# VectorE's part of a first-layer step emitted behind the next step's evacuations

## The chip, the cores and the metric

One Trainium2 chip, one of its cores. The metric is the device time of one execution in microseconds (us), taken without the profiler unless said; the profile's span is some 2 us shorter than that time (243.4 beside 245.14 in the profiled execution of the kernel before). A program on one core has no die to compare with, so executions are told apart by their span and by the mean clock granted to TensorE, which the records give for every execution.

## The reference

Chunked attention (4 batches, 8 heads, 768 rows of 64; chunks of 32 queries see 16 rows to the left, 8 to the right and 8 memory rows), then a two-layer MLP on the 3072 x 512 result:

```python
x = attention(q, k, v, mem_k, mem_v)       # (3072, 512)
h = x @ w_in                               # 512 -> 2048
s = np.sin(alpha * h)
g = h + s * s / (alpha + 1e-09)
out = g @ w_out                            # 2048 -> 512
```

## The kernel before

Matmul and transpose results land in PSUM, the memory that TensorE writes; a buffer there is free again once an engine has copied or used up what it holds (its evacuation). The kernel works through four blocks, one per batch. For each there is an attention burst that fills xT, then the first layer in 16 steps (ft), each of which makes 128 rows of g; the second layer of the block is a stream of matmuls handed out in small portions between other work. In the first layer of blocks 1 and 2 the q and k of the *next* block are transposed as well, one piece every other step. The PSUM buffers in use are three two-bank ones ("big") and two one-bank ones ("sm"). hT is a step's first-layer result, tt_a a transpose, kTi and qT the copies made of it, o and o_sb a second-layer output and its copy; hT 14 or sin 9 below is that of ft 14 or 9.

```python
big = ctx.enter_context(tc.tile_pool(name="big", bufs=3, space=bass.MemoryType.PSUM))
smp = ctx.enter_context(tc.tile_pool(name="smp", bufs=2, space=bass.MemoryType.PSUM))
# ...
def t_k(kb, hp):                            # piece for k; t_q is the same with a copy on ScalarE
    t = t_tile()                            # in blocks 1 and 2: tt_a, from the two "sm" buffers
    # ... six transposes on TensorE into t ...
    nc.vector.tensor_copy(kTi[...], t[...])             # large
    # ... and two small tensor_copy, all three on VectorE
# ...
def l1(i, ft, xT, gT, sq, split=False):     # the case without split
    hT = big.tile([P, 2, 512], F32, name="hT", tag="big")
    # ... 8 matmuls into hT ...
    nc.scalar.activation(u[:], hT[:, :, 0:HALF], ACTF.Sin, scale=alpha_sb[:, ft:ft + 1])
    if sq == "A":
        nc.scalar.activation(s2[:], u[:], ACTF.Square)
    else:
        (nc.vector if sq == "D" else nc.gpsimd).tensor_tensor(
            out=s2[:], in0=u[:], in1=u[:], op=ALU.mult)
    nc.vector.scalar_tensor_tensor(         # gT = s2 / alpha + hT, releases hT
        out=gv, in0=s2[:], scalar=inv_alpha[:, ft:ft + 1],
        in1=hT[:, :, 0:HALF], op0=ALU.mult, op1=ALU.add)
# ...
def l2(i, gT, last=False):
    for s in range(NSUB):
        o = smp.tile([P, d_model], F32, name="o", tag="sm")
        # ... 16 matmuls into o, handed out one by one ...
        if s % 2 == 0:
            nc.vector.tensor_copy(o_sb[:], o[:])        # releases o
        else:
            nc.scalar.copy(o_sb[:], o[:])
# ...
for ft in range(FT):
    sq = ("ADADADAAADADADAA" if i == 0 else "ADAAPDADADAPADAD")[ft]
    if 1 <= ft:
        stream.take(3 if last else 2)       # second-layer matmuls, and o_sb when one is full
    if 0 < i < B - 1 and ft in at_ft:       # ft even
        piece(at_ft[ft])                    # k at ft = 0, 4, 8, 12; q between
    # ...
    l1(i, ft, xT, gT, sq, i == 0 and ft in (3, 7, 11))
```

The order in which instructions are written is the order in which each engine gets them.

The softmax here doesn't subtract the row's maximum and nothing guards it: scores larger than these inputs give would overflow.

Of the kernel before, what the change touches and what calls it, by code (L numbers as in the profile page):

```python
# [9 lines left out]
P = 128  # L10
# [6 lines left out]
ALU = mybir.AluOpType  # L17
# [28 lines left out]
def kernel(  # L46
# [12 lines left out]
    nc = tc.nc  # L59
    B, H, S, D = q.shape  # L60
# [8 lines left out]
    HALF = S // 2  # L69
# [28 lines left out]
    inv_alpha = consts.tile([P, FT], F32, name="inv_alpha")  # L98
# [13 lines left out]
    def load_qk(b):  # L112
        kb, qb = alloc_qk()
        for src, dst in ((k, kb), (q, qb)):
            nc.gpsimd.dma_start(
                dst[:].rearrange("p h r d -> p h (r d)"),
                src[b].rearrange("h (p r) d -> p h (r d)", p=P),
            )
        return kb, qb
# [32 lines left out]
    def put_memv(b):  # L152
        nc.vector.tensor_copy(
            vws[b % 2][64:72, :, :, 0:D],
            memv_st[64:72, b].unsqueeze(2).to_broadcast([NM, H, NJ, D]),
        )

    def put_memk(b):
        nc.vector.tensor_copy(
            kTi[:, :, 24:KW].rearrange("p g (j c) -> p g j c", c=104)[:, :, :, 40:40 + NM],  # L160
            memkT[:, :, NM * b:NM * b + NM].unsqueeze(2).to_broadcast([P, HP, NJ, NM]),
        )
# [28 lines left out]
    for c0, c1, thr, val in (  # L191
# [4 lines left out]
            out=biasm[:, c0:c1], in_=biasm[:, c0:c1],  # L196
# [27 lines left out]
    def pair_up(src, hp, eng=None):  # L224
        pr = blk.tile([P, 6, 2, D], BF, name="pr")
        (eng or nc.gpsimd.tensor_copy)(  # L226
            pr[:].rearrange("p r e d -> p e r d"), src[:, 2 * hp:2 * hp + 2]
        )
        return pr
# [81 lines left out]
    def burst(b, stream, shares, lag):  # L311

        xT = xp.tile([P, KT, S], BF, name="xT")
        ptl, xbl = {}, {}
        for s in range(NJ + lag + 1):
            n = shares[s] if s < len(shares) else 0
            if s < NJ:
                ptl[s] = qk_exp(s)
            if b == 0:
                spin(1)  # L320
            stream.take(n // 3, True)
            if 0 <= s - lag < NJ:
                xbl[s - lag] = pv(b, s - lag, ptl.pop(s - lag))
                if b == 0:
                    xbl[s - lag] = (xbl[s - lag][0], None)
            stream.take((n + 1) // 3, True)
            if 0 <= s - lag - 1 < NJ:
                xt(xT, s - lag - 1, *xbl.pop(s - lag - 1))
            stream.take((n + 2) // 3, True)
        return xT  # L330


    def l1(i, ft, xT, gT, sq, split=False):
        if split:
            hts = [smp.tile([P, 512], F32, name="hs", tag="sm") for _ in range(2)]
        else:
            hT = big.tile([P, 2, 512], F32, name="hT", tag="big")
            hts = [hT[:, 0], hT[:, 1]]
        for kt in range(KT):
            for hf in range(2):  # L340
                nc.tensor.matmul(  # L341
                    hts[hf][:, 0:HALF],
                    w_in_sb[:, kt, P * ft:P * ft + P],
                    xT[:, kt, HALF * hf:HALF * hf + HALF],
                    start=(kt == 0), stop=(kt == KT - 1),
                )
        u = mlp.tile([P, 2, HALF], F32, name="u")
        if split:
            for hf in range(2):
                nc.scalar.activation(  # L350
                    u[:, hf], hts[hf][:, 0:HALF], ACTF.Sin, scale=alpha_sb[:, ft:ft + 1])
        else:
            nc.scalar.activation(u[:], hT[:, :, 0:HALF], ACTF.Sin, scale=alpha_sb[:, ft:ft + 1])  # L353
        s2 = mlp.tile([P, 2, HALF], F32, name="s2")
        if sq == "A":
            nc.scalar.activation(s2[:], u[:], ACTF.Square)  # L356
        else:
            (nc.vector if sq == "D" else nc.gpsimd).tensor_tensor(  # L358
                out=s2[:], in0=u[:], in1=u[:], op=ALU.mult)
        gv = gT[:, ft, :].rearrange("p (e c) -> p e c", e=2)  # L360
        for hf in range(2):
            if split:
                nc.vector.scalar_tensor_tensor(
                    out=gv[:, hf], in0=s2[:, hf], scalar=inv_alpha[:, ft:ft + 1],
                    in1=hts[hf][:, 0:HALF], op0=ALU.mult, op1=ALU.add)
            elif hf == 0:
                nc.vector.scalar_tensor_tensor(  # L367
                    out=gv, in0=s2[:], scalar=inv_alpha[:, ft:ft + 1],
                    in1=hT[:, :, 0:HALF], op0=ALU.mult, op1=ALU.add)

    def l2(i, gT, last=False):
        for s in range(NSUB):
            o = smp.tile([P, d_model], F32, name="o", tag="sm")
            end = last and s == NSUB - 1
            o_sb = mlp.tile([P, d_model], F32, name="o_sb")
            row = S * i + P * s
            if end:
                oh = [o, smp.tile([P, d_model], F32, name="o", tag="sm")]
                for c in range(2):
                    cs = slice(256 * c, 256 * c + 256)  # L380
                    for ft in range(FT):
                        nc.tensor.matmul(  # L382
                            oh[c][:, 0:256], gT[:, ft, P * s:P * s + P], w_out_sb[:, ft, cs],
                            start=(ft == 0), stop=(ft == FT - 1),
                        )
                    if c == 0:
                        nc.scalar.copy(o_sb[:, cs], oh[c][:, 0:256])
                    else:
                        nc.vector.tensor_copy(o_sb[:, cs], oh[c][:, 0:256])
                    nc.sync.dma_start(out[row:row + P, cs], o_sb[:, cs])  # L390
            else:
                for ft in range(FT):
                    nc.tensor.matmul(  # L393
                        o[:], gT[:, ft, P * s:P * s + P], w_out_sb[:, ft, :],
                        start=(ft == 0), stop=(ft == FT - 1),
                    )
                    if ft < FT - 1:
                        yield False
                if s % 2 == 0:
                    nc.vector.tensor_copy(o_sb[:], o[:])  # L400
                else:
                    nc.scalar.copy(o_sb[:], o[:])  # L402
                nc.sync.dma_start(out[row:row + P, :], o_sb[:])
            yield True
# [31 lines left out]
    xT = burst(0, stream, (), 2)  # L436
# [3 lines left out]
    for i in range(B):  # L440
        gT = gp.tile([P, FT, S], BF, name="gT")
        last = i == B - 1
        at_ft = {2 * n: n for n in range(8)}
        pieces = []
        if not last:
            srcs = [(kq_next[n % 2], n // 2) for n in range(2 * HP)]
        state["pools"] = 1

        def pair_to(n):
            while len(pieces) < min(n, 2 * HP):  # L450
                pieces.append(pair_up(*srcs[len(pieces)], nc.vector.tensor_copy if i == 0 and len(pieces) % 2 == 0 else None))

        def piece(n):
            pair_to(n + 3)
            (t_k if n % 2 == 0 else t_q)(pieces[n], n // 2)

        if 0 < i < B - 1:
            pair_to(2)
        for ft in range(FT):
            sq = ("ADADADAAADADADAA" if i == 0 else "ADAAPDADADAPADAD")[ft]  # L460
            if 1 <= ft:
                stream.take(3 if last else 2)
            if 0 < i < B - 1 and ft in at_ft:
                piece(at_ft[ft])
            if i == 0 and ft == 14:
                pair_to(3)
            l1(i, ft, xT, gT, sq, i == 0 and ft in (3, 7, 11))
        stream.add(l2(i, gT, last))
        if not last:
            if i == 0:  # L470
                state["pools"], state["t"] = 3, 0
                stream.take(4)
                for n in range(2 * HP):
                    piece(n)
                    stream.take(3, True)
            if i + 2 < B:
                kq_next = load_qk(i + 2)
            if i == 0:
                xT = burst(i + 1, stream, (3, 3, 3, 4, 4, 4, 4, 4, 4, 4, 5, 5), 3)
            else:  # L480
                xT = burst(i + 1, stream, (16, 8, 6, 6, 6, 5, 5, 5, 5, 5), 1)
            if i + 2 < B:
                put_memk(i + 2)
            stream.take(3)
            if i + 2 < B:
                load_v_all(i + 2)
                put_memv(i + 2)
# [31 lines left out]
```

## Time and profile before

| | before |
|---|---|
| median of the plain runs (lowest to highest) | 243.68 us (243.36 to 245.46) |
| span of the profiled execution | 243.4 us |
| mean granted clock of it | 0.986 |
| TensorE idle, first layer of block 1 (79 to 113 us) | 3.88 of 34 us |
| TensorE idle, first layer of block 2 (133 to 168 us) | 3.30 of 35 us |

The lines are in the prediction. To read them: PE is TensorE and PEld its weight loads, DVE is VectorE, ACT ScalarE, POOL GpSimd. In a list of waits, the engine and instruction on the left stood idle until the one behind the arrow was done (us in total, times, longest). In a list by time, the columns are start, us, engine, line, operation, output and inputs, count, and in brackets the idle time of that engine just before and what ended it.

### The profile page before, as it was taken

The numbers are of one execution on the slowest core, as the hardware profiler recorded it, in microseconds if no ns is written. First come the engines' busy times: TensorE is split into PE (matmuls) and PEld (weight loads), VectorE is DVE, ScalarE is ACT, GpSimd is POOL, SyncE is SP. The second block draws the span as 40 slices with busy tenths as digits, with TensorE's granted clock in tenths as the row PEclk, the third lists the DMA queues.
The fourth block names the chain that finished last, engine by engine and source line by source line (L and its number), as shares of the span: only waits on it lengthen the run. The fifth ranks groups of instructions, "written<-read, shape, count | busy, mean of one in ns | idle before, by whom it ended". The sixth has DMA issues, their size and how long they took to land.

```text
span 243.4 us, 4498 instructions
## 1 busy us (share of the span) xinstructions
PE 222.6 (91%) x1785; PEld 123.0 (51%) x1785; DVE 160.2 (66%) x287; ACT 154.7 (64%) x237; POOL 73.3 (30%) x96
## 2 busy tenths in 40 slices
PE   6798899989989899898999997998999999899994
PEld 2355565545445455454455653554455555453453
DVE  3496969999268658969457775868657267876101
ACT  3489599973975467798464784678765675871000
POOL 8899865214712114157200222120000002020000
PEclk9799999999999999999999997999999999999999
DMA  6999999999999610109992101001111101101122
GB/s 75 165 130 83 161 194 204 207 198 134 190 208 134 74 46 0 44 4 181 154 151 66 46 0 43 0 3 43 46 43 47 43 0 46 43 0 40 46 89 86
DMA packets 53852, 21.11 MB, mean 87 GB/s; under 512 B 36296, under 2 KB 50888, under 8 KB 53832
## 3 DMA queue, kind: packets, MB, share of 16 engines
q0 software_dynamic: 47616, 14.40, 70.7%
q1 hardware_dynamic: 6216, 6.43, 8.9%
q8 instruction: 14, 0.23, 0.4%
q14 instruction: 6, 0.05, 0.1%
HBM read 28.91 MB, written 6.29 MB: 145 GB/s over the span
## 4 chain that ended last, share of the span: by engine, by line
PE 48%; DVE 20%; ACT 12%; issue 12%; POOL 3%; DMA 2%; POOLq 1%; DVEq 0%; ACTq 0%
PE o L393 26%; PE hT L341 10%; DVE gT L367 8%; DVE s L358 5%; ACT pt L275 4%; ACT u L353 4%; ACT s L356 3%; PE ot L288 3%; PE sc L266 3%; POOL s L358 2%; DMA q_bf<-in_q_dram 2%; DVE kTi L243 2%; PE ot L306 2%; PE o L382 1%; DVE x_blk L293 1%
## 5 line engine op out<-in xcount | busy, mean ns | idle before, releaser
L393 PE MATMUL o<-w_out_sb,gT 128*128 128x512 bf16 x368 | 99.0, 381 | 0.7 <-DVE gT L367 0.4
L341 PE MATMUL hT<-xT,w_in_sb 128*128 128x384 bf16 x488 | 88.8, 329 | 3.9 <-DVE gT L367 3.6
L367 DVE SCALAR_TENSOR_TENSOR gT<-s,inv_alpha,hT 128x768 bf16<-128x768 f32 x61 | 61.2, 1012 | 30.0 <-ACT s L356 21.6
L353 ACT ACTIVATE u<-hT,alpha_sb 128x768 f32<-128x768 f32 x61 | 54.7, 898 | 28.3 <-PE hT L341 27.1
L341 PEld LDWEIGHTS <-w_in_sb 128*128 128x128 bf16 x512 | 49.8, 99 | 39.7 <-issue 7.4
L275 ACT ACTIVATE pt<-sc,biasm 128x256 bf16<-128x256 f32 x96 | 37.6, 492 | 13.0 <-PE sc L266 13.0
L393 PEld LDWEIGHTS <-gT 128*128 128x128 bf16 x368 | 31.9, 98 | 26.9 <-DVE gT L367 1.4
L358 POOL TENSOR_TENSOR s<-u 128x768 f32<-128x768 f32 x6 | 8.8, 1465 | 73.7 <-ACT u L353 73.7
L356 ACT ACTIVATE s<-u 128x768 f32<-128x768 f32 x34 | 28.7, 843 | 1.1
L358 DVE TENSOR_TENSOR s<-u 128x768 f32<-128x768 f32 x24 | 24.7, 1029 | 0.9 <-ACT u L353 0.8
L226 POOL COPY pr<-q_bf 128x768 bf16<-128x768 bf16 x12 | 10.1, 838 | 43.7 <-PE tt_a L242 27.4
L293 DVE TENSOR_TENSOR x_blk<-ot,rinv 96x512 bf16<-96x512 f32 x32 | 22.0, 686 | 1.1
L292 DVE RECIPROCAL rinv<-ot 96x8 f32<-96x8 f32 x32 | 6.4, 201 | 20.1 <-PE ot L288 19.8
L402 ACT COPY o_sb<-o 128x512 f32<-128x512 f32 x11 | 6.4, 585 | 20.0 <-PE o L393 20.0
L400 DVE COPY o_sb<-o 128x512 f32<-128x512 f32 x12 | 8.2, 687 | 15.4 <-PE o L393 15.4
L288 PEld LDWEIGHTS <-pt 128*128 128x128 bf16 x256 | 11.9, 97 | 7.2 <-issue 2.3
L171 PE MATMUL z<-zeros 128*128 128x512 bf16 x37 | 13.9, 463 | 1.3 <-DVE zeros L165 1.3
L288 PE MATMUL ot<-vw,pt 128*128 128x65 bf16 x256 | 13.0, 193 | 0.8 <-ACT pt L275 0.6
L266 PEld LDWEIGHTS <-kTi 64*128 64x128 bf16 x256 | 6.9, 94 | 13.0 <-issue 6.6
L266 PE MATMUL sc<-qT,kTi 64*128 64x96 bf16 x256 | 11.4, 205 | 1.8 <-ACT pt L275 1.2
L257 PEld LDWEIGHTS <-pr 128*128 128x128 bf16 x96 | 6.6, 100 | 12.5 <-issue 8.0
L306 PEld LDWEIGHTS <-x_blk 96*128 96x128 bf16 x128 | 8.4, 97 | 6.6 <-DVE x_blk L293 1.6
(66 smaller groups left out, 182.1 us busy)
## 6 DMA issues: line engine op xcount, KB each, us to landing
out_dram<-o_sb SPq DMA_DIRECT2D x23, 256.0 KB, 2.1
k_bf<-in_k_dram POOLq DMA_DIRECT2D x3, 768.0 KB, 8.6
q_bf<-in_q_dram POOLq DMA_DIRECT2D x3, 768.0 KB, 12.6
vw<-in_v_dram POOLq DMA_DIRECT2D x6, 384.0 KB, 17.4
w_in_sb<-in_moe_w_in_dram POOLq DMA_DIRECT2D x8, 256.0 KB, 8.3
w_out_sb<-in_moe_w_out_dram POOLq DMA_DIRECT2D x4, 512.0 KB, 18.7
k_bf<-in_k_dram POOLq DMA_DIRECT2D x4, 192.0 KB, 6.2
q_bf<-in_q_dram POOLq DMA_DIRECT2D x4, 192.0 KB, 6.7
```

The lines of the kernel that those rows point to most:

```text
L171: nc.tensor.matmul(z[:], zeros[:, 0:P], zeros[:])
L266: nc.tensor.matmul(sc[:, e, QW * hp:QW * hp + QW], kTi[64 * e:64 * e + 64, hp, 104 * j:104 * j + P], qT[64 * e:64 * e + 64, hp, QW * j:QW ...
L275: nc.scalar.activation(pt[:, 0:H * QW].rearrange("p (g e c) -> p e g c", g=4, e=2)[:, :, :, 32 * m:32 * m + 32], sc[:, :, 0:4 * QW].rearra ...
L288: nc.tensor.matmul(otv[:, h // 4, h % 4, :], pt[:, QW * h:QW * h + P], vws[b % 2][:, h, j, 0:D + 1])
L293: nc.vector.tensor_tensor(out=x_blk[:].rearrange("p (g e) d -> p g e d", g=2), in0=otv[0:QW, :, :, 0:D], in1=rv.unsqueeze(3).to_broadcast( ...
L306: nc.tensor.transpose(xtp[:, kt, :], x_blk[:, 2 * kt:2 * kt + 2, :].rearrange("p e d -> p (e d)"), ident[0:QW, 0:QW])
L341: nc.tensor.matmul(hts[hf][:, 0:HALF], w_in_sb[:, kt, P * ft:P * ft + P], xT[:, kt, HALF * hf:HALF * hf + HALF], start=(kt == 0), stop=(kt ...
L353: nc.scalar.activation(u[:], hT[:, :, 0:HALF], ACTF.Sin, scale=alpha_sb[:, ft:ft + 1])
L356: nc.scalar.activation(s2[:], u[:], ACTF.Square)
L358: (nc.vector if sq == "D" else nc.gpsimd).tensor_tensor(out=s2[:], in0=u[:], in1=u[:], op=ALU.mult)
L367: nc.vector.scalar_tensor_tensor(out=gv, in0=s2[:], scalar=inv_alpha[:, ft:ft + 1], in1=hT[:, :, 0:HALF], op0=ALU.mult, op1=ALU.add)
L393: nc.tensor.matmul(o[:], gT[:, ft, P * s:P * s + P], w_out_sb[:, ft, :], start=(ft == 0), stop=(ft == FT - 1),)
```

## The change

The intent: VectorE's queue runs in order. When a finished second-layer output (o) or a finished transpose (tt_a) waits for its copy, and the copy stands behind a gT instruction whose input is not there yet, TensorE soon waits for the PSUM buffer. So l1 now returns VectorE's part (square where it is VectorE's, then gT) as a function, which is called after the *next* step's copies have been emitted. TensorE, ScalarE, GpSimd and the DMA queues keep their order exactly.

```diff
-        else:
-            (nc.vector if sq == "D" else nc.gpsimd).tensor_tensor(
-                out=s2[:], in0=u[:], in1=u[:], op=ALU.mult)
-        gv = gT[:, ft, :].rearrange("p (e c) -> p e c", e=2)
-        ... gT on VectorE (scalar_tensor_tensor) ...
+        elif sq == "P":
+            nc.gpsimd.tensor_tensor(out=s2[:], in0=u[:], in1=u[:], op=ALU.mult)
+
+        def finish():
+            if sq == "D":
+                nc.vector.tensor_tensor(out=s2[:], in0=u[:], in1=u[:], op=ALU.mult)
+            gv = gT[:, ft, :].rearrange("p (e c) -> p e c", e=2)
+            ... gT on VectorE, unchanged ...
+
+        return finish
@@ the loop over ft
+        finish = None
         for ft in range(FT):
             ... stream.take, piece, pair_to ...
-            l1(i, ft, xT, gT, sq, i == 0 and ft in (3, 7, 11))
+            if finish is not None:
+                finish()
+            finish = l1(i, ft, xT, gT, sq, i == 0 and ft in (3, 7, 11))
+        finish()
```

## The prediction

> **What bounds the kernel now.** I read four views in this order: the page of the profile, the busy time by stage, the list of waits in two of those stages, and the instructions in order of time there. The page first:
>
> ```profile
> PE 222.6 (91%) x1785; PEld 123.0 (51%) x1785; DVE 160.2 (66%) x287; ACT 154.7 (64%) x237; POOL 73.3 (30%) x96
> ```
>
> TensorE (PE) works 91% of the span, VectorE (DVE) 66%. The change takes no work from any engine, so it can gain only where PE stands still, and only where PE stands still for something VectorE does. Next, busy time by stage. I cut the span by the program's blocks: 79 to 113 us is the first layer of block 1 (16 steps "ft"), 133 to 168 that of block 2, 190 to 222 that of block 3; the two between are attention bursts.
>
> ```profile
> 79.00:113.00 34.00, 30.12 (x214) 17.89 (x213) 25.89 (x36) 24.17 (x30) 12.50 (x13) 1.00 0.29 47
> 113.00:133.00 20.00, 20.00 (x216) 10.35 (x215) 12.57 (x28) 11.51 (x27) 2.99 (x4) 1.00 1.90 140
> 133.00:168.00 35.00, 31.70 (x207) 18.13 (x205) 25.22 (x35) 23.72 (x29) 7.12 (x7) 0.95 0.06 23
> 168.00:190.00 22.00, 21.96 (x234) 11.29 (x232) 13.97 (x30) 14.28 (x30) 0.00 (x0) 1.00 0.10 38
> 190.00:222.00 32.00, 30.85 (x174) 16.71 (x171) 21.99 (x24) 22.43 (x27) 2.93 (x2) 1.00 0.07 25
> ```
>
> The columns are length, then busy us of PE, PEld, DVE, ACT, POOL, then granted PE clock. The bursts are full (20.00 of 20.00, 21.96 of 22.00): a gain won before them passes through as a shift. The first layers of blocks 1 and 2 hold 3.88 and 3.30 us of idle PE; block 2 also has a granted clock of 0.95. What PE waits for there, block 1 and then block 2:
>
> ```profile
> PE tt_a L257 <- DVE o_sb L400: 1.4, 1, 1.4
> PE hT L341 <- DVE gT L367: 1.0, 2, 0.5
> PE tt_a L257 <- DVE kTi L249: 1.0, 1, 1.0
> ...
> PE sc L266 <- DVE gT L367: 0.5, 1, 0.5
> ```
>
> ```profile
> PE tt_a L257 <- DVE o_sb L400: 1.7, 1, 1.7
> PE tt_a L257 <- DVE kTi L249: 1.4, 2, 0.9
> ...
> PEld L393 <- DVE kTi L249: 0.5, 1, 0.5
> ```
>
> All of block 1's 3.88 us, and nearly all of block 2's, are waits for VectorE to release a PSUM buffer. The largest share goes to tt_a (the next block's transposes), which shares a two-buffer pool with the second layer's output o. Its release is the copy o_sb, or the kTi copies of the previous transposes. Why the copies come late shows in order of time, block 2:
>
> ```profile
> 143.38 0.59 PE L393 MATMUL o<-w_out_sb,gT 128*128 128x512 bf16 x2
> ...
> 146.06 1.01 DVE L367 SCALAR_TENSOR_TENSOR gT<-s,inv_alpha,hT 128x768 bf16<-128x768 f32 x1 [0.73 <-POOL s L358]
> 146.99 0.68 DVE L400 COPY o_sb<-o 128x512 f32<-128x512 f32 x1
> ...
> 147.72 0.49 PE L257 MATMUL tt_a<-ident,pr 128*128 128x128 bf16 x6 [1.73 <-DVE o_sb L400]
> ...
> 148.06 2.46 PE L341 MATMUL hT<-xT,w_in_sb 128*128 128x384 bf16 x8
> ```
>
> The output o was complete by 143.97, but its copy stood in VectorE's queue behind a gT instruction that waited for the square made on POOL until 146.06. PE waited from 145.99 to 147.72, and the eight matmuls after it took 2.46 us instead of 1.46: the clock dropped.
>
> **The Trainium skill.** "PSUM — Partial Sum Buffer", section "Engine vs sequencer instructions", says that the VectorE queue is strict FIFO; the lines above agree, a copy ready at 143.97 ran at 146.99 behind a waiting one. "TensorE: Matmul & The Clock Gate", "What's actually happening", says that the PE clock halves after an idle window of about 3.4 us, counted by a free-running window. The trace agrees on the halving (one 128x384 matmul per 0.32 us at 148 to 150 us, 0.16 elsewhere), not on the need for a long gap: 1.73 us, after 0.28 us shortly before, was enough, while 1.35 us at 85.69 was not. "SBUF — State Buffer", "Who interferes with whom", says that a VectorE instruction with two SBUF inputs is held up by a GpSimd instruction reading SBUF. The trace agrees: the VectorE square takes 0.95 us alone, but 1.38 and 1.50 at 94.74 and 153.96, beside POOL's pr copies.
>
> **The change part by part.** A comparison of both programs' orders shows that PE, ACT, POOL and SP keep theirs exactly; only VectorE's changes, in ten places. In each, copies move ahead of the previous step's gT instruction (0.93 us from start to start), and, where that step squares on VectorE, ahead of its square (0.88) too. No duration is added or removed. I worked each place out by hand, with the durations of the trace and its hand-over times: an activation starts 1.50 us after its hT's first matmul; hT needs the gT of three steps earlier, for there are three such buffers.
>
> Block 0, one place: two pr copies (0.62) go ahead of square and gT of ft 13. PE waits 0.43 now for those copies; afterwards the first tt_b waits for the buffer of hT 13, released at about 53.25, so it starts at about 53.3 instead of 53.18. Sum +0.1.
>
> Block 1, four places.
> - o_sb ahead of gT 0. o is complete at 82.61, VectorE is free from 82.32 until gT 0 gets its square at 84.03; the 0.69 us copy fits in that hole. The wait of 1.35 goes and nothing is delayed.
> - kTi (1.08 with its two small copies) ahead of gT 3: gT 3 is about 0.3 late, harmless.
> - kTi ahead of square 7 and gT 7. Now it ends at 101.47 and PE waits 1.00. Afterwards, on the shifted clock, it ends near 97.7, tt_a wants it at 99.1: the wait goes. gT 7 ends near 99.7 and hT 10 could start at 99.44: a new wait of 0.3.
> - kTi ahead of gT 11. From sin 9 on ACT takes over: ACT runs from about 99.8 to 110.2 without a hole (six sines, three squares, two qT copies; at present it idles 1.6 us there), and the gT's that release hT wait for it. New PE waits of about 0.3 (hT 13), 0.8 (hT 14) and 0.25 (scores).
> The first score matmuls start at about 109.65, now 112.56: 2.9 saved. From ACT's side: sin 9 comes 1.27 earlier and 1.6 of idle goes, again 2.9.
>
> Block 2, four places.
> - kTi ahead of gT 3: 0.28 of PE wait at 145.11 goes.
> - o_sb ahead of gT 4: o_sb runs at 144.53 to 145.22, in the hole before the POOL square, and tt_a starts at 145.54 instead of 147.72. 2.18 with the 0.28.
> - kTi ahead of square 7 and gT 7: wait of 0.73 (157.00 to 157.73) goes.
> - kTi ahead of gT 11: 1.05 (164.89 to 165.94) goes. ACT has more air here; a new wait of about 0.65 stays before the scores, for gT 13.
> hT 8 and hT 10 find their buffers free within 0.1 us of wanting them. Sum 2.18 + 0.73 + 1.05 - 0.65 = 3.3, say 3.4 with rounding of the hand-overs. The clock drop behind the long wait cost a further 1.65 in this execution, and should go with it.
>
> Block 3, one place: o_sb ahead of gT 3, with both output buffers free and PE full. Nothing.
>
> Sum: 0.1 - 2.9 - 3.4 = -6.2 us, or -7.8 against an execution with the clock drop. The profiled execution was timed at 245.14 us, the three plain runs at 243.68, 243.36 and 245.46. The two near 245.3 are 1.8 longer than the others, about the 1.65 of the drop, so I take the median 243.68 to be without it (an inference, not shown). Prediction: 243.68 - 6.2 = 237.5.
>
> **The rivals.**
> - gT later, buffers later: moving copies ahead delays gT, gT releases hT, and PE waits there instead. For it: block 1's 1.0 us of hT waits for gT. Against: the o_sb copies run in holes where gT waits anyway, and kTi delays gT by 1.08 only where hT is needed about 1 us later. If it took half, 240.5.
> - Only the o_sb moves pay: -1.35 and -2.18 give 240.2, if ACT (24.17 of 34.00 busy, and solid at the end) holds all the rest. For it: my block 1 ends ACT-bound. Against: block 2 does not, and there the kTi waits are PE's only ones.
> - The gain is larger: if the median had the clock drop in it, -7.8 gives 235.9.
> - A later stage gives it back. Against: the bursts are full of PE work, and the loads for them were issued in an earlier block.
>
> **Range and chances.** The terms that only take away a visible wait (1.35, 2.18) are firm; the four kTi terms carry an error of perhaps 0.5 each, nearly all on the low side. So 235.8 to 239.7. The bound of 2% lies at 238.8, 1.3 us above the prediction: faster 0.82, within 2% 0.17, slower 0.01.
>
> **What would show it.** In the profile afterwards: no PE wait of tt_a for o_sb in either block; kTi waits under 0.3 in all; granted clock 1.00 in block 2; small new waits of hT or the scores for gT, about 1.4 in block 1 and 0.7 in block 2; the distance from the first hT of block 1 to its first score matmul 28.9 instead of 31.8, in block 2 about 29.5 instead of 34.5. It is wrong if waits of hT for gT exceed 2 us a block, or if the same copies still end the waits of tt_a.

## The result, and the profile after

| | before | after |
|---|---|---|
| median of 4 plain runs each | 243.85 us | 236.78 us |
| lowest to highest | 243.36 to 245.46 | 236.55 to 237.25 |
| span of the profiled execution | 243.4 us | 234.8 us |
| granted clock of it | 0.986 | 1.00 |

The ratio is 0.9701 (95% interval 0.9653 to 0.9750). Ratios here are the mean time of one kernel's fast runs over the mean of the other's of the same rounds, so not quite the ratio of the medians quoted beside them.

The busy times of the changed kernel, the line of its page that answers to the first one in the prediction. (Its PE count is lower because a few matmul records are missing from this trace: 1759 against 1785 weight loads.)

```profile
PE 217.1 (92%) x1759; PEld 122.3 (52%) x1785; DVE 160.8 (69%) x287; ACT 153.8 (66%) x237; POOL 72.1 (31%) x96
```

VectorE and the others have nearly the same busy time as before, in a shorter span: the 8.6 us less of span are idle time, and time at a lower clock, taken away. Where, by stage: the first layers of block 1 and block 2 (columns: length, then busy us of PE, PEld, DVE, ACT, POOL, then clock, DMA share, GB/s):

```profile
79.00:110.00 31.00, 29.88 (x212) 18.19 (x214) 26.08 (x36) 23.42 (x29) 11.89 (x12) 1.00 0.31 49
...
130.00:160.00 30.00, 29.84 (x204) 18.02 (x205) 25.04 (x35) 23.63 (x30) 7.02 (x7) 1.00 0.07 27
```

The idle time of TensorE is down to 1.12 us of 31 and 0.16 of 30 (a last wait, before the scores at 160.58, falls just behind it), and the clock of block 2 is 1.00. What TensorE still waits for, in block 1 (79 to 110 us) and then in block 2 (128 to 162 us). The gT instruction is now at line 370, o_sb at 405, o at 398:

```profile
PE hT L341 <- DVE gT L370: 0.7, 2, 0.5
PEld L341 <- DVE gT L370: 0.7, 1, 0.7
```

```profile
PE sc L266 <- DVE gT L370: 0.6, 1, 0.6
```

No wait of tt_a is left, neither for o_sb nor for kTi. In their place stand waits for gT, as they must if gT is now the later one, but they are much shorter. (The wait shown for PEld is not a further one: it is the longer of PE's two, for the weight loads go with the same matmuls.) The stretch of block 2 that the prediction showed, in order of time:

```profile
139.97 0.59 PE L398 MATMUL o<-w_out_sb,gT 128*128 128x512 bf16 x2
...
141.04 0.68 DVE L405 COPY o_sb<-o 128x512 f32<-128x512 f32 x1
...
142.14 0.50 PE L257 MATMUL tt_a<-ident,pr 128*128 128x128 bf16 x6
142.47 1.46 PE L341 MATMUL hT<-xT,w_in_sb 128*128 128x384 bf16 x8
...
142.66 1.02 DVE L370 SCALAR_TENSOR_TENSOR gT<-s,inv_alpha,hT 128x768 bf16<-128x768 f32 x1 [0.94 <-POOL s L358]
```

The output o is complete at 140.56; its copy starts at 141.04, behind the gT of the step before but ahead of the one that waits for POOL, and so in VectorE's hole. Nothing in brackets stands behind tt_a any more: it follows the second-layer matmuls without a gap. The eight matmuls take 1.46 us and not 2.46, and gT still runs the moment its POOL square is there: putting the copy first cost it nothing.

A good measure for all that follows is the length of a block's first layer on TensorE: from the first hT matmul to the first score matmul of the next burst. For blocks 1 and 2 it repeats to within 0.02 us between executions of the same order, where no clock drop falls into it. For block 0 it does not: with its old order it lasted 32.77, 32.99, 33.45 and 32.77 us in the traces of the kernel before, the control kernel and two more looks at the latter.

| | before (profiled) | after |
|---|---|---|
| block 0 (28.94 to 61.71; 28.70 to 61.60) | 32.77 | 32.90 |
| block 1 (80.72 to 112.56; 80.62 to 109.15) | 31.84 | 28.53 |
| block 2 (134.48 to 168.96; 131.08 to 160.58) | 34.48 | 29.50 |

Blocks 1 and 2 give 3.31 and 4.98 of the 8.6 us of span; the bursts between them last 19.02 and 21.93 as before (19.01, 21.92), the third 21.58 (21.79). The rest lies ahead of block 1.

### The profile page after: what moved, and what is told of

Its sections match the earlier page's. It is cut to its first block, busy times and chain, and to the rows that moved or that the text cites. A ratio compares the mean times of both kernels' runs of the same rounds, so it can differ in the third digit from the quotient of the medians.

```text
span 234.8 us, 4467 instructions
## 1 busy us (share of the span) xinstructions
PE 217.1 (92%) x1759; PEld 122.3 (52%) x1785; DVE 160.8 (69%) x287; ACT 153.8 (66%) x237; POOL 72.1 (31%) x96
## 4 chain that ended last, share of the span: by engine, by line
PE 60%; DVE 15%; ACT 11%; issue 7%; DMA 3%; POOL 2%; POOLq 1%; DVEq 0%; ACTq 0%
PE o L398 29%; PE hT L341 19%; DVE gT L370 6%; ACT pt L275 4%; ACT u L353 3%; DMA q_bf<-in_q_dram 3%; PE ot L288 3%; DVE s L362 3%; PE sc L266 3%; ACT s L356 2%; PE ot L306 2%; DVE x_blk L293 2%; PE o L387 1%; PE tt_a L257 1%; PE tt_a L242 1%
## 5 line engine op out<-in xcount | busy, mean ns | idle before, releaser
L398 PE MATMUL o<-w_out_sb,gT 128*128 128x512 bf16 x343 | 93.1, 380 | 2.0 <-issue 0.5
L341 PE MATMUL hT<-xT,w_in_sb 128*128 128x384 bf16 x488 | 87.3, 326 | 3.8 <-DVE gT L370 3.4
L341 PEld LDWEIGHTS <-w_in_sb 128*128 128x128 bf16 x512 | 49.3, 98 | 38.5 <-issue 4.7
L171 PE MATMUL z<-zeros 128*128 128x512 bf16 x36 | 13.2, 451 | 1.3 <-DVE zeros L165 1.3
L226 POOL COPY pr<-k_bf 128x768 bf16<-128x768 bf16 x8 | 6.6, 826 | 11.2 <-PE tt_a L257 5.8
```

The lines of the kernel that those rows point to most:

```text
L171: nc.tensor.matmul(z[:], zeros[:, 0:P], zeros[:])
L226: (eng or nc.gpsimd.tensor_copy)(pr[:].rearrange("p r e d -> p e r d"), src[:, 2 * hp:2 * hp + 2])
L341: nc.tensor.matmul(hts[hf][:, 0:HALF], w_in_sb[:, kt, P * ft:P * ft + P], xT[:, kt, HALF * hf:HALF * hf + HALF], start=(kt == 0), stop=(kt ...
L398: nc.tensor.matmul(o[:], gT[:, ft, P * s:P * s + P], w_out_sb[:, ft, :], start=(ft == 0), stop=(ft == FT - 1),)
```

## The experiments

All kernels but the two marked wrong are the changed source, with one line that says where the deferred part is still emitted late; elsewhere it is emitted at its old place:

```diff
+            late = ...                       # see each experiment
+            if finish is not None and not late:
+                finish()
             if 1 <= ft:
                 stream.take(3 if last else 2)
             ... piece, pair_to ...
-            if finish is not None:
+            if finish is not None and late:
                 finish()
```

### control: nothing late

```diff
+            late = False
```

> The changed source with every deferred part emitted at its old place: every engine's order is that of the kernel before, so both theories expect a ratio of 1.00 within 0.5%. What it adds is the granted clock and span of several executions of the old order. Theory A (the long wait for o_sb in block 2 brings a clock drop of about 1.65 us in some executions only) expects a mixture: some executions near clock 1.00 and span about 241.8, some near 0.986 and span about 243.4. Theory B (the drop is there every time) expects all near 0.986 and 243.4.

Measured: 243.85 us median of 6, ratio 0.9978 (0.9932 to 1.0024) to the kernel before: writing the source in two parts changes nothing that these runs can tell. First layers of its profiled execution (clock 1.00): block 1 31.85, block 2 32.80. So block 2 of the old order lasts 32.8 us at full clock, and the 34.48 of the first trace hold 1.68 us of clock drop. Its six executions, span and clock: 241.4, 241.5 and 241.5 at 1.00, 241.6 at 0.991, 243.0 at 0.993, 243.1 at 0.986. That is theory A's mixture. The kernel before showed it too: of the 22 executions measured, 12 had a span of 242.5 or more, and the 7 at a clock of 1.00 had 240.9 to 241.8 and times of 243.05 to 243.57.

### osb_only: the two o_sb copies alone

```diff
+            late = (i, ft) in ((1, 1), (2, 5))
```

> Only the two o_sb copies of blocks 1 and 2 move ahead. Additive theory: block 1 gives 1.35, block 2 gives 1.9 (145.82 to 147.72 of the old trace, its kTi wait of 0.28 stays), together 3.25 us, plus the clock drop of 1.65 in those executions that had it: 3.3 to 4.9 us, about 239 to 240.5. The waits of tt_a for kTi stay (about 1.0 in block 1, 0.6 plus 0.9 in block 2). Rival (o_sb and the clock are everything, the kTi moves only shift waits): 6.5 to 7 us, like the whole change. Rival (ACT or gT take up what o_sb frees): under 2 us.

Measured: 240.26 us, before 244.06; ratio 0.983 (0.978 to 0.988). Block 1 30.34, block 2 31.05: 1.51 and 1.75 us against control. TensorE's waits for tt_a in its block 2 (129 to 170 us) show what went and what stayed:

```profile
PE tt_a L257 <- DVE kTi L249: 1.4, 2, 0.9
...
PEld L398 <- DVE kTi L249: 0.5, 1, 0.5
```

The line for o_sb is gone, those for kTi stand unchanged. The additive theory holds, and both rivals fall; but that the sum fits so well (3.25 expected, 3.26 measured) is luck, for block 1 gave 0.16 more than the 1.35 expected and block 2 0.15 less than the 1.9.

### kti_only: the six kTi groups alone

```diff
+            late = i in (1, 2) and ft in (4, 8, 12)
```

> Only the six kTi groups of blocks 1 and 2 move ahead, o_sb stays behind gT. Additive theory: block 1 gives 3.3 (its whole gain of the changed trace) minus 1.35, about 1.95; block 2 gives 0.73 + 1.05 - 0.6 = about 1.2, since the 0.28 before o is swallowed by the o_sb wait, which grows to about 2.0: together about 3.1 us, near 240.7, with the o_sb waits and the clock drop still there. Rival (o_sb is everything): under 1 us. The rival that gT comes later and stalls hT expects more than 2 us of hT waiting for gT in a block.

Measured: 240.63 us, ratio 0.983 (0.9779 to 0.988) over its four fast runs; two more executions (243.77 and 244.5, clocks 0.979 and 0.984) were slow and are left out. Their spans, 242.4 and 242.0, lie 3.3 to 4.1 above the other four (238.3 to 238.7), which would fit two late clock drops of 1.68 each (an estimate; neither was traced). The ratio flatters this kernel a little: its fast runs have no such drop, while those of the kernel before include it. Block 1 30.04, block 2 31.69: 1.81 and 1.11 us, together 2.92 where 3.1 was expected. In its block 2:

```profile
PE tt_a L257 <- DVE o_sb L405: 2.0, 1, 2.0
...
PE sc L266 <- DVE gT L370: 0.6, 1, 0.6
```

Here is the small interaction in figures: the wait for o_sb grew from 1.7 to 2.0, because the 0.28 us that the first kTi group frees is waited away again at the next tt_a; o_sb's own time is set by the square on POOL. The rival of gT stalling hT falls: those waits stay as small as in the whole change.

With control as the base the parts sum up so: block 1 1.51 + 1.81 = 3.32, the whole change 3.32; block 2 1.75 + 1.11 = 2.86, the whole change 3.30. The missing 0.44 in block 2 needs both moves.

### block1: all of block 1, nothing elsewhere

```diff
+            late = i == 1
```

> All four moves of block 1, none elsewhere. Additive theory: first hT to first scores in block 1 is 28.5 us as in the changed kernel (31.8 before), block 2 stays at about 34.5 with the drop or 32.8 without: 3.3 us, near 240.5. A rival in which the bursts or the later blocks give gains back expects less than 2.5 us of total gain although block 1 is as short.

Measured: 241.03 us, ratio 0.9854 (0.9805 to 0.9904). Block 1 28.51, block 2 32.80, the gain of block 1 with block 2 untouched. The median gain is 3.0 us, between the 2.5 of the rival and the 3.3 expected; its two executions at a clock of 1.00 had spans of 237.6 and 238.6 (control's three 241.4 to 241.5), so 2.8 to 3.9. No later stage gives it back.

### blocks12: without the moves of blocks 0 and 3

```diff
+            late = i in (1, 2)
```

> The change without its moves in block 0 (pr copies) and block 3 (o_sb). Theory: those two are worth +0.1 and 0, so the time is that of the whole change within 0.3 us, about 236.6 to 236.8, and 6.5 to 7.4 us under the kernel before; in no execution a second clock drop (no span over 236). Rival (the pr copies or block 3 gave part of the 7 us): 238 or more.

Measured: 237.08 us, before 244.96; ratio 0.9703 (0.966 to 0.9745), that of the whole change is 0.9701. Blocks 1 and 2 28.52 and 29.51. The moves in blocks 0 and 3 are worth nothing that these runs can tell. The other half of the expectation failed: one of the six executions had a span of 236.4 at a clock of 0.986, the others 234.8 to 235.4.

### osb_block2: one copy

```diff
+            late = (i, ft) == (2, 5)
```

> Only the o_sb copy of block 2 moves. Additive theory: the block's first layer goes from 32.8 us (no drop) to 31.05, block 1 stays at 31.84: 1.75 us, undropped executions at a span near 239.7. If the 1.7 us wait for o_sb is what brings the clock drop, no execution has a span over 241.0; if the drop comes from elsewhere (the kTi waits, block 1), some 4 in 10 executions still lie 1.5 to 2 us above the rest.

Measured: 242.61 us, before 244.96; ratio 0.9935 (0.9884 to 0.9985). Block 1 31.85, block 2 31.05: one copy moved, 1.75 us off its block, as expected. But the spans were 239.5, 239.8, 240.3, 241.3, 241.8 and 242.1, the last three at clocks of 0.993, 0.986 and 0.984. Three long executions of six are still there, so the long wait for o_sb in block 2 is not all that brings the drop.

### Four more looks for the clock drop

> A second look at the kernel with only block 2's o_sb moved, to see in a trace where its clock drop falls, should it have one (3 of 6 executions had a span 1.5 to 2.5 us longer). If the drop follows the PE waits, it lies behind another wait: that for o_sb in block 1 (near 86 us, 1.35 us) or those for kTi in block 2 (near 155 and 163 us). If it lies where PE did not wait, waits are not its cause.

> The same kernel again, for about one execution in two shows the drop: if it has one, it lies behind the o_sb wait of block 1 or the kTi waits of block 2 by the theory that idle PE brings it.

> A second look at the old order. If the long o_sb wait of block 2 is the usual place of the drop, a dropped execution (span over 242.5) shows half clock at about 148 to 152 us, as the first trace did; if not, elsewhere.

> The old order once more, for one execution in two shows no drop: a dropped one shows half clock at about 148 to 152 us if the long o_sb wait is its usual place, and elsewhere if it is not.

Measured: spans 240.3, 240.0, 241.5 and 241.7, clocks 0.993, 0.993, 1.00 and 0.991; first layers of blocks 1 and 2 31.85 and 31.05, twice, then 31.84 and 32.79, 31.85 and 32.80. None caught a drop in the later part. What they show is that there are two kinds. The clock of the first look at osb_block2 (0.993) comes from one stretch at half clock during the start-up, at 8 to 12 us; at the later stretch it is full (the clock is the figure before the last two):

```profile
8.00:12.00 4.00, 3.07 (x20) 1.87 (x21) 1.47 (x7) 2.36 (x3) 3.30 (x12) 0.57 1.32 198
148.00:152.00 4.00, 4.00 (x29) 2.38 (x28) 3.70 (x4) 2.67 (x4) 0.83 (x1) 1.00 0.00 0
```

The first trace of the kernel before had both:

```profile
8.00:12.00 4.00, 3.23 (x21) 1.89 (x22) 1.38 (x4) 2.34 (x3) 3.30 (x12) 0.57 1.28 189
148.00:152.00 4.00, 4.00 (x18) 1.91 (x16) 1.55 (x2) 2.15 (x3) 0.87 (x1) 0.57 0.17 66
```

Asked in narrower windows, both stretches of this trace are 3.41 us long at a clock of 0.50 (8.41 to 11.82 and 148.35 to 151.76). Over a span of 243.4 us one such stretch lowers the mean clock by 0.007: a mean of 0.993 goes with one, 0.986 with two, wherever they fall, so it is the span that tells a late drop from an early one. The early one costs little (control_look2 had it, and its span of 241.7 is 0.2 over that of control_look1); the late one costs 1.68 us by the stage table. Its place was seen in one trace only.

### nosq11 and nosq12: what sets the end of block 1

Both give a wrong result (relative error 0.13): in the changed kernel the square of one step of block 1 is left out, and gT takes the sine in its place.

```diff
+        elif sq == "N":
+            s2 = u
...
+            if (i, ft) == (1, 11):           # nosq12: (1, 12)
+                sq = "N"
```

> WRONG RESULT ON PURPOSE: the changed kernel with the POOL square of ft 11 in block 1 left out (gT takes the sine in its place). If ACT without a hole sets the end of block 1, as the prediction had it, first hT to first scores stays at 28.5 us and the wait of hT 14 for gT is only moved to another instruction. If the POOL square sets it, the wait of hT 14 (0.7) goes to about 0.3 and the stage to about 28.0.

> WRONG RESULT ON PURPOSE: the changed kernel with the ACT square of ft 12 in block 1 left out, 0.85 us less of ACT work in the stretch that the prediction calls ACT-bound. If ACT sets the end of block 1, the stage becomes about 0.5 to 0.85 us shorter than 28.5; if VectorE and the POOL square do, it stays within 0.15 of 28.5.

Measured: block 1 lasts 28.27 us without the POOL square of ft 11, and 28.53 without the ScalarE square of ft 12, where the changed kernel has 28.53. So 0.84 us less of ScalarE work, late in the stretch that the prediction called bound by ScalarE, is worth nothing; the POOL square is worth 0.26, half of what I expected. And the burst after it then lasts 22.34 us where the changed kernel has 21.93, so the whole kernel gains nothing by it. How, in order of time; first the changed kernel:

```profile
97.32 0.90 ACT L353 ACTIVATE u<-hT,alpha_sb 128x768 f32<-128x768 f32 x1 [1.10 <-PE hT L341]
...
102.70 0.88 ACT L353 ACTIVATE u<-hT,alpha_sb 128x768 f32<-128x768 f32 x1
...
103.67 1.47 POOL L358 TENSOR_TENSOR s<-u 128x768 f32<-128x768 f32 x1 [6.73 <-ACT u L353]
...
104.03 0.90 ACT L353 ACTIVATE u<-hT,alpha_sb 128x768 f32<-128x768 f32 x1 [0.44 <-PE hT L341]
...
105.17 1.94 DVE L370 SCALAR_TENSOR_TENSOR gT<-s,inv_alpha,hT 128x768 bf16<-128x768 f32 x2 [0.33 <-POOL s L358]
...
106.24 2.77 PE L341 MATMUL hT<-xT,w_in_sb 128*128 128x384 bf16 x16 [0.55 <-DVE gT L370]
...
107.03 0.95 DVE L362 TENSOR_TENSOR s<-u 128x768 f32<-128x768 f32 x1
...
107.81 0.90 ACT L353 ACTIVATE u<-hT,alpha_sb 128x768 f32<-128x768 f32 x1 [0.53 <-PE hT L341]
108.08 1.01 DVE L370 SCALAR_TENSOR_TENSOR gT<-s,inv_alpha,hT 128x768 bf16<-128x768 f32 x1
...
109.15 0.35 PE L266 MATMUL sc<-qT,kTi 64*128 64x96 bf16 x8
```

hT 14 waits for gT 11, gT 11 for the square on POOL, and that square for sin 11 (102.70), the last of eight ScalarE instructions that follow one another without a hole from 97.32 to 103.58. After it ScalarE waits twice for TensorE (0.44 and 0.53), so from there on it is not what holds the stage. VectorE is: from 105.17 it goes without a hole through gT 11, gT 12, the square of ft 13 and gT 13, which ends at 109.09, and the scores, which need its buffer, start at 109.15.

Without the ScalarE square of ft 12, which comes after sin 11, the wait of hT 14 is the same:

```profile
106.33 2.77 PE L341 MATMUL hT<-xT,w_in_sb 128*128 128x384 bf16 x16 [0.55 <-DVE gT L372]
```

Without the POOL square:

```profile
104.60 0.31 DVE L249 COPY kTi<-tt_a 128x48 bf16<-128x48 bf16 x2
...
104.83 1.00 DVE L372 SCALAR_TENSOR_TENSOR gT<-u,inv_alpha,hT 128x768 bf16<-128x768 f32 x1
...
108.97 0.35 PE L266 MATMUL sc<-qT,kTi 64*128 64x96 bf16 x8 [0.30 <-DVE gT L372]
```

gT 11 now follows straight on the kTi copies, 0.42 earlier counted from the start of the stage, and a new wait of 0.30 appears before the scores, again for gT: behind the square VectorE itself is next. What these two runs do not test is the ScalarE work before sin 11, which stands ahead of both: of the POOL square, and of gT 10, which waited 0.35 for a ScalarE square before those kTi copies (102.90). (With the square gone POOL also issues its next loads earlier, so this is not a change of one thing only.)

## Why the prediction was right

The median, 236.78, lies in the range of 235.8 to 239.7, 0.7 under the predicted 237.5. The base it was counted from, 243.68, was the median of three runs; the medians of eleven runs later were 244.06 and 244.96, so that it lay near the time without a late drop (243.37, below) was partly luck. Step by step:

- *What bounds the kernel.* Right. TensorE's waits for VectorE's copies were the whole matter: they are gone from the lists, and each part moved alone takes away its own waits and shortens its blocks (3.26 and 2.92 us in all).
- *Block 0, +0.1.* Not shown. It measured +0.13 (32.77 to 32.90), but the same old order lasted from 32.77 to 33.45 in four traces. Leaving the move out changes nothing in the total that can be told.
- *Block 1, -2.9.* Measured -3.31. This is the term that was mis-sized. Of the 0.4, 0.16 lies in the o_sb term, which was called firm (1.35 predicted, 1.51 measured by osb_only), and 0.26 in the kTi terms (1.55 left for them, 1.81 measured by kti_only). The step in it was "From sin 9 on ACT takes over: ACT runs from about 99.8 to 110.2 without a hole". In the trace sin 9 starts at 99.46, but the run without a hole ends at 103.58; then ScalarE waits 0.44 and 0.53, and removing 0.84 us of its work there shortens nothing. The path that ended the stage was VectorE's: counted from the first hT, sin 13 comes 2.26 us earlier than before (108.06 then, 105.71 now), but gT 13, which the scores wait for, 3.32 earlier (111.50, 108.08): gT 11 comes 2.32 earlier (107.59, 105.17), and the kTi copies no longer stand between it and gT 12. The waits listed were of the right kind and too large: hT 10 0.18 (0.3 predicted), hT 13 none (0.3), hT 14 0.55 (0.8), the scores none (0.25). That of hT 14 is for the square on POOL, and this one began when ScalarE's run without a hole ended; how much that ScalarE work is worth stays open.
- *The sums for block 1.* The prediction's two did not agree: its four new waits, 1.65 together, taken from 3.88 of idle time leave a gain of 2.2, and it went by ScalarE's path, which gave 2.9. (That path holds seven sines, 9 to 15, not six.)
- *Block 2, -3.4 at full clock.* Measured 32.80 to 29.50, -3.30. The remaining wait before the scores is 0.58, predicted 0.65. The sum is right to 0.1; inside it the o_sb term was 0.15 too large (1.90 without the 0.28, measured 1.75) and the gain that needs both moves 0.16 too small (0.28, measured 0.44), which cancels.
- *The clock drop, 1.65 us in some executions.* Its size is right (1.68), and that the quick plain runs are those without it is now shown by spans and clocks. That the long wait brought it ("was enough") and that it "should go with" that wait was too simple: with the wait gone from block 2 alone, three of six executions were still long, and the changed order without the moves of blocks 0 and 3 had one of six; and three traces of the old order have the same 1.7 us wait and no late drop. Of the kernel before, 12 of 22 executions were long, of the changed kernel none of four; so the drop became rarer, and part of the measured 7.07 is due to that. Executions at a clock of 1.00 tell the rest: seven of before have a mean of 243.37, three of after 236.70, 6.7 apart. What starts a late drop stays open.
- *The rivals.* "gT later, buffers later": the waits of hT and of the scores for gT did not grow in block 1 (1.0 and 0.5 before, 0.7 in all after), and in block 2 there is one new one of 0.6; that is far from half of the gain. "Only the o_sb moves pay" is refuted by kti_only: the two kinds share the gain almost evenly (3.26 and 2.92). "A later stage gives it back" is refuted by block1 and by the lengths of the bursts.

## What to carry to other kernels

On an engine whose queue runs in order, an instruction that waits for a slow producer delays everything emitted behind it; put the copies that release a scarce PSUM buffer, and whose input is already there, ahead of it. Look for a wait of TensorE on a copy, then look in order of time at what stood before that copy in its own queue and what *that* waited for: where the copy fitted in the hole, as o_sb did here, the move cost nothing. Then follow the chain through all engines to its end: here ScalarE, POOL and VectorE held the same stage one after the other, and a busy ScalarE in its middle was not what ended it. Judge such a change by the length of the stage on the engine that paces it, which for blocks 1 and 2 here repeats to 0.02 us, and count clock drops apart, for they shift the median of a few runs by more than some of the parts.

## What the Trainium skill lacked or had wrong

- "TensorE: Matmul & The Clock Gate", "What's actually happening": the page ties the half clock to about 3.4 us of idle. In the one late drop that was traced, TensorE had waited 1.73 us, shortly after a wait of some 0.28, and then ran at half clock for 3.41 us at a cost of 1.68. That the wait started it is not shown. The page speaks elsewhere of frequent short idles that make the clock swing, but gives no length for them, and does not say that the same program can lose the clock in the middle of its work in some executions and not in others: the kernel before had long executions in 12 of 22, and the same wait (1.7 us) in three traces of the old order brought no drop.
- No page gives a figure for the loss when an in-order VectorE queue holds a PSUM copy behind a waiting instruction. Here one such copy, begun 3.0 us after its input was ready (143.97 to 146.99), cost 1.75 us of block 2 at full clock (32.80 to 31.05 when it alone was moved).
